# Routing constants in three parts, matrices ahead of a batch's scatters, seven first layers ahead

## The chip, the cores and the metric

The kernel runs on one core of a Trainium2 chip. A core has five engines that run side by side, each with its own instruction queue: TensorE (PE, matrix products and transposes), VectorE (DVE), ScalarE (ACT), GpSimd (POOL) and SyncE (SP, which here only issues transfers). Transfers (DMAs) are issued from POOL's, SP's and ACT's queues and run on 16 shared DMA engines. The metric is the device time of one execution in microseconds; less is better.

## The reference

Chunked attention with memory keys, followed by a mixture of experts with a dense residual. Sizes: 4 batches, 8 heads, 768 positions, head size 64; so 3072 tokens of 512 numbers; 8 experts with a hidden width of 512.

```python
for c in range(seq // 32):                       # chunks of 32 queries
    k_full = [mem_k (8 rows), k from 16 before the chunk to 8 behind it]
    a = softmax(q_c @ k_full.T / 8)
    out[c] = a @ v_full
x = out as [3072, 512]
y_dense = relu(x @ w1_dense) @ w2_dense
logits = x @ w_gate                              # 8 experts
e = argmax(logits); g = softmax(logits)[e]
y = y_dense + g * (relu(x @ w1[e]) @ w2[e])      # each token by its own expert e
```

## The kernel before

**Attention.** The loop runs over 16 pairs of heads (`NPAIR`), four pairs to a batch of 768 tokens. It is software-pipelined: in the iteration of pair i TensorE does the scores of pair i + 1, the transposes of pair i + 2 and the values of pair i; DVE does the maximum (L409), the subtraction (L415), the scaling of the values (`scaled`, L447 and L448), one copy of key columns (L376) and one of v's two head copies (L351); ScalarE does the exponential and PSUM copies; POOL does the other v copy and issues the loads of q and k. SyncE loads v.

The order on each engine is written out by hand: `tc.manual_schedule` keeps the instructions of each engine in the order in which the program calls them, and an instruction that waits holds up all that stands behind it on its engine.

**Routing.** As a batch's four pairs are done, its logits are summed up. In the second pair of the next batch (`routing`, pairs 5, 9 and 13) `logits`, `choose`, `ranks` and `rank` work out each token's expert and its row in a table in device memory, `x_reg`. Then POOL writes the batch's 768 rows there with six indirect DMAs of 128 rows (`rows_out`, L587), each one behind a tiny memset (`apart`, L578). Those of batches 0 and 1 are spread over later pairs by `row_out`; those of batch 2 come all at the end of pair 13, each followed by half a weight matrix (`half_w`); those of batch 3 come behind the attention (from "for t in range(T): rows_out(B - 1, (t,))"). The routing needs constants (ones, triangles, counters). `constants()` makes them at the end of the iteration of pair 1: DVE memsets (L733 to L747), POOL iotas (L122), and a DVE cast of each iota (L124), one by one.

**Tiles.** Tokens are processed in tiles of 128 that belong to one expert. In the last pair `list_a` works out the first 11 tiles (`NA`) from whole tiles of batches 0 to 2. SyncE reads their addresses into registers (`bases`) and fetches each from `x_reg` (`fetch`, L188); these fetches wait for the rows of batches 0 to 2, not for those of batch 3. `transposed` (L202 to L207) turns a tile, `dense_first` (L216, L222) and `dense_second` (L232, L235) do the dense layers. The other tiles (16, `NFIX`) are listed by `list_b` when batch 3's rows are placed, and follow in a second loop.

**Weights.** All matrices are loaded by POOL with a cast to 16 bits, in the order of `w_todo`: the two dense ones, then `w1` of the 8 experts, then `w2`. A `half_w` issues half a matrix (L779), `load_w` a whole one (L115). The last twelve are issued in a loop behind the rows of batch 3; there a tiny POOL copy (L964) waits until the matrix before the previous one has landed, so two are under way.

**Experts.** `experts(lo, hi, ahead)` runs for 27 tiles: `staged` copies the tile's `w1` matrix to a fixed place (DVE, L929), `expert_first` does the first layer, `expert_second` (L942, L947) the second, then POOL runs a memset of 256 numbers (`pause`, L581) and an indirect DMA (L951) that writes 128 rows of the output. The second layers read `w2` at a place known only at run time, so the first of them waits for all of `w2`. First layers run `ahead` of the second ones, by this formula:

```python
want = min(hi, lo + ahead + -(-(k + 1 - lo) * (hi - lo - ahead) // (hi - lo)))
```

Before the second layer of tile `k`, first layers up to `want` have been issued. Results `y` have a ring of 6 buffers, each free again when its output DMA has landed.

Of the kernel before, what the change touches and what calls it, by code (L numbers as in the profile page):

```python
# [11 lines left out]
F32 = mybir.dt.float32  # L12
# [8 lines left out]
def kernel(  # L21
# [90 lines left out]
    def load_w(src_ap, dst, parts=1):  # L112
        n = DT // parts
        for t in range(0, DT, n):
# [2 lines left out]
                src_ap[t * 128:(t + n) * 128].rearrange("(t p) m -> p t m", p=128),  # L117
            )

    def iota_f32(n, name, base=0, step=1, cm=0):  # L120
        ti = r_pool.tile([128, n], I32, name=name + "_i")
        nc.gpsimd.iota(ti, pattern=[[step, n]], base=base, channel_multiplier=cm)  # L122
        tf = r_pool.tile([128, n], F32, name=name)
        nc.vector.tensor_copy(tf, ti)  # L124
        return tf

    xT_A = keep.tile([128, NA, DT, 128], BF16, name="xT_A")
# [372 lines left out]
    def gate_add(pi):  # L500
        b, hp = divmod(pi, NP)
        lgT = bat[b]["lgT"]
        if hp == 0:
            nc.vector.tensor_copy(lgT, g_ps[:96, :])
        else:
            nc.vector.tensor_tensor(lgT, lgT, g_ps[:96, :], ALU.add)

    def logits(b):
        lgT = bat[b]["lgT"]
        lg_ps = bank()  # L510
        for j in range(2):
            nc.tensor.transpose(
                lg_ps[:, j * 96:(j + 1) * 96], lgT[:, j * 128:(j + 1) * 128],
                identity_f32[:96, :96],
            )
        bat[b]["lg"] = lg_ps
# [25 lines left out]
    def ranks(b):  # L542

        oh = bat[b]["oh"]
        rk_t = bank()
        rk_ps = rk_t[:, :T * E].rearrange("p (t e) -> p t e", e=E)
        nc.tensor.matmul(rk_ps, upper, oh, start=True, stop=False)
        for t in range(T - 1):
            nc.tensor.matmul(
                rk_ps[:, t + 1:, :], ones,  # L550
                oh[:, t:t + 1, :].to_broadcast([128, T - 1 - t, E]),
                start=False, stop=False,
            )
# [23 lines left out]
    def apart():  # L577
        nc.gpsimd.memset(scratch, 0.0)  # L578

    def pause():  # L580
        nc.gpsimd.memset(idle, 0.0)  # L581

    def rows_out(b, ts=range(T)):
        rec, row_i = bat[b]["rec"], bat[b]["row"]
# [142 lines left out]
        clear_v(i, nc.vector)  # L727
    load_v(2)

    def constants():  # L730
        out_ = {}
        ones = r_pool.tile([128, 128], BF16, name="ones")
        nc.vector.memset(ones, 1.0)  # L733
        upper = r_pool.tile([128, 128], BF16, name="upper")
        nc.gpsimd.affine_select(
            upper, ones, pattern=[[1, 128]], compare_op=ALU.is_ge, fill=0.0,
            base=-1, channel_multiplier=-1,
        )
        upto = r_pool.tile([128, E, E], F32, name="upto")
# [7 lines left out]
        nc.vector.memset(fill[:, IC:], FAR)  # L747
        slot_no = iota_f32(NB, "slot_no")
# [6 lines left out]
        reg0 = iota_f32(E, "reg0", base=128, step=ROWS)  # L755
        nc.vector.tensor_copy(seen_bf, reg25)
        return ones, upper, upto, slot_no, slot128, desc, pcol, tok, base_a, reg25, reg0

    transpose_qk(0)
    scores(0)  # L760
# [3 lines left out]
    copy_v(0, 0, nc.gpsimd)  # L764
    transpose_qk(1)
    copy_v(0, 1, nc.vector)
    probs_back(0)
    w_todo = [(moe_w1_dense, w1d_sb), (moe_w2_dense, w2d_sb)]
    for e in range(E):
# [15 lines left out]
    for i in range(NPAIR):  # L785
        b, hp = divmod(i, NP)
        routing = hp == 1 and b > 0
        if routing:
            gate_add(i - 2)
        if i + 4 < NPAIR:  # L790
            load_qk(i + 4, "q")
        if i + 3 < NPAIR:
            load_v(i + 3)
        if i + 1 < NPAIR:
            row_out()
            if i < NPAIR - 2:
                copy_v(i + 1, 0, nc.gpsimd)
            row_out()
            scores(i + 1)
        if i + 4 < NPAIR:  # L800
            load_qk(i + 4, "k")
        if i < 2:
            clear_side(i + 2, nc.gpsimd)
        if routing:
            logits(b - 1)
        if i:
            scaled(i - 1)
            copy_v(i, 1, nc.scalar if routing else nc.vector)
        if routing:
            choose(b - 1)  # L810
        if i:
            probs_back(i)
            gate_part(i - 1)
        if i + 1 < NPAIR:
            maximum(i + 1)
            softmax(i + 1)
        if i > 1 and not routing:
            gate_add(i - 2)
        if i == NPAIR - 1:
            parts = list_a()  # L820
            next(parts)
            bases(0, 6)
            for s in range(6):
                fetch(s)
            bases(6, NA)
        values(i, range(TB))
        if i + 2 < NPAIR:
            transpose_qk(i + 2)
        values(i, range(TB, T))
        if routing:  # L830
            ranks(b - 1)
        if i:
            record(i - 1)
            if i == NPAIR - 2:
                copy_v(i + 1, 0, nc.scalar)
            gate_sum(i - 1)
        if routing:
            rank(b - 1)
        if i == NPAIR - 4:
            half_w()  # L840
            half_w()
        if routing:
            rows_todo += [(b - 1, (t,)) for t in range(T)]
        if i == NPAIR - 3:
            while rows_todo:
                row_out()
                half_w()
        if i == 1:
            (ones, upper, upto, slot_no, slot128, desc, pcol, tok, base_a, reg25,
             reg0) = constants()  # L850
        if i == NPAIR - 3:
            fill_out()

# [6 lines left out]
    gate_sum(last_p)  # L860
    record(last_p)
    gate_add(last_p)
    transposed(0)
    logits(B - 1)
    dense_first(0)
    choose(B - 1)
    transposed(1)
# [3 lines left out]
    rank(B - 1)  # L871
    for t in range(T):
        rows_out(B - 1, (t,))
        if t < 2:
            half_w()
        elif t < T - 1:
            pause()
    dense_second(0)
    fetch(7)
# [57 lines left out]
    def expert_second(s):  # L937
        h_e = h_of.pop(s)
        place, py = y_bank()
        e = e_pe.pop(s)  # L940
        for f in range(FT):
            written(place, nc.tensor.matmul(  # L942
                py, h_e[:, f, :], w2_all[:, bass.ds(e, 1), f, :],
                start=(f == 0), stop=(f == FT - 1),
            ))
        y = l_work.tile([128, D_moe], F32, tag="y", name="y", bufs=6)
        was_read(place, nc.vector.scalar_tensor_tensor(  # L947
            y, py, meta[:, s:s + 1], yd_of[s], op0=ALU.mult, op1=ALU.add
        ))
        pause()  # L950
        inst = nc.gpsimd.indirect_dma_start(  # L951
            out, bass.IndirectOffsetOnAxis(ap=dst_i[:, s:s + 1], axis=0), y, None,
            bounds_check=N_tokens - 1, oob_is_err=False,
        )
        tc.declare_no_dep(inst.ins, group="outs", reason="every row is written once")
        tc.add_to_no_dep_group("outs", inst.ins)
# [41 lines left out]
            expert_second(k)  # L998

    turn["banks"] = 4  # L1000
    experts(0, last, NA)
    n_used = nc.values_load(  # L1002
        et_i[0:1, NS:NS + 1], min_val=0, max_val=NB,
        skip_runtime_bounds_check_because="a count of tiles",
# [40 lines left out]
```

## Time and profile before

| what | value |
|---|---|
| median of 3 runs | 251.78 us (249.72 to 254.38) |
| the profiled execution's own time | 251.12 us |
| its span, first to last instruction | 249.3 us |
| mean granted TensorE clock | 0.964 |
| busy PE / DVE / ACT / POOL | 198.0 / 157.6 / 135.0 / 146.5 us |
| moved by DMA | 38.57 MB, mean 155 GB/s |
| attention | to about 125 us |
| dense tiles | about 128 to 187 us |
| experts | about 187 us to the end |

Busy times are sums over a program whose stages have different limits, so none of them alone says what a change is worth; the stages and the waits within them do. TensorE's matmuls are pipelined, so its busy time is not time at its peak. The granted clock is the share of full speed that the chip let TensorE run at.

### The profile page before, as it was taken

To read this page: it belongs to the slowest core of one execution; us is meant where nothing else is said; L and a number is where in the kernel's file an instruction comes from. 1 tells how busy PE (TensorE), PEld (TensorE's weight loads), DVE (VectorE), ACT (ScalarE), POOL (GpSimd) and SP (SyncE) were. 2 spreads that over 40 slices of the span, in tenths; PEclk is the share of its full clock that TensorE was granted. 3 is DMA by queue.
4 is the path that set the end of the run, shared out by engine and by line. 5 is a ranking of instruction groups with operands and counts; after the bars stand their busy time and mean duration, and the time that the engine had idled before them with its cause. 6 is when DMAs were issued, how large, how long until landed. Compare 5 with 4: busy or idle time off the path is not lost. (4 is left out here: it accounts for less than half of the span.)

```text
span 249.3 us, 7849 instructions
## 1 busy us (share of the span) xinstructions
PE 198.0 (79%) x3147; PEld 147.8 (59%) x3147; DVE 157.6 (63%) x372; ACT 135.0 (54%) x205; POOL 146.5 (59%) x209
## 2 busy tenths in 40 slices
PE   1578498978887887686548998999999999998810
PEld 1466376756765665564336776777769866665500
DVE  4568679879888988877634542222236577887510
ACT  6265666896878667887314464566566512212100
POOL 8939973317996599428712841122131079988881
PEclk9999859999999999999988999999999999999985
DMA  5999999998999999948988959999989024332432
GB/s 91 184 193 134 160 157 158 148 146 158 167 172 202 163 139 170 164 163 122 212 187 158 203 84 245 234 196 203 145 138 163 6 84 168 148 137 113 163 127 87
DMA packets 59895, 38.57 MB, mean 155 GB/s; under 512 B 35662, under 2 KB 57550, under 8 KB 59856
## 3 DMA queue, kind: packets, MB, share of 16 engines
q0 software_dynamic: 21600, 25.20, 57.1%
q1 hardware_dynamic: 37216, 11.77, 28.4%
q10 hardware_dynamic: 1040, 1.06, 1.3%
q8 instruction: 27, 0.44, 0.8%
q14 instruction: 12, 0.10, 0.1%
HBM read 43.22 MB, written 11.30 MB: 219 GB/s over the span
## 5 line engine op out<-in xcount | busy, mean ns | idle before, releaser
L587 POOL DMA_INDIRECT x_reg<-rec,row_i x24 | 27.8, 1160 | 28.0 <-ACT rec L478 12.8
L951 POOL DMA_INDIRECT out_dram<-y,dst_i x27 | 30.0, 1113 | 17.0 <-DVE y L947 13.6
L436 PE MATMUL av<-vw,at 128*32 128x130 f32 x768 | 30.1, 292 | 8.3 <-issue 3.7
L436 PEld LDWEIGHTS av<-vw,at 128*32 128x32 f32 x768 | 21.4, 115 | 15.3 <-issue 10.0
L351 POOL COPY vw<-vw 24x1536 f32<-24x1536 f32 x15 | 22.5, 1500 | 13.2 <-DMA vw<-in_v_dram 12.7
L222 ACT ACTIVATE h<-sc 128x512 bf16<-128x512 f32 x27 | 16.1, 597 | 24.8 <-PE sc L216 22.9
L216 PEld LDWEIGHTS <-w_st 128*128 128x128 bf16 x432 | 25.3, 98 | 5.6 <-DVE w_st L929 1.7
L216 PEld LDWEIGHTS <-w1d 128*128 128x128 bf16 x432 | 26.3, 100 | 2.1 <-issue 1.7
L222 ACT ACTIVATE xT_B<-sc 128x512 bf16<-128x512 f32 x16 | 9.6, 597 | 28.8 <-PE sc L216 20.1
L420 ACT ACTIVATE a<-dif 128x768 f32<-128x768 f32 x16 | 13.5, 845 | 18.3 <-DVE dif L415 15.6
L929 DVE COPY w_st<-w_all 128x2048 bf16 x27 | 19.0, 709 | 6.3 <-PE sc L216 5.0
L205 DVE COPY xT_B<-tp 128x512 bf16<-128x512 bf16 x16 | 6.8, 425 | 24.1 <-PE tp L202 24.1
L376 DVE COPY kbd<-tp 64x768 bf16<-64x768 bf16 x16 | 15.2, 947 | 8.3 <-PE tp L363 7.3
L232 PE MATMUL av<-w2d,h 128*128 128x512 bf16 x72 | 18.5, 379 | 0.1
L964 POOL CAST scratch<-w_all 1x1 f32<-1x1 bf16 x10 | 1.7, 175 | 28.6 <-DMA w_all<-in_moe_w_dram 28.6
L468 PE MATMUL tp<-identity_f,x 128*128 128x128 f32 x96 | 14.1, 285 | 4.9 <-DVE x L448 4.8
L216 PE MATMUL sc<-xT_B,w_st 128*128 128x128 bf16 x256 | 16.9, 219 | 1.0 <-DVE w_st L929 0.6
L428 ACT COPY at<-at_ps 128x768 f32<-128x768 f32 x16 | 12.8, 799 | 9.0 <-PE at_ps L426 7.8
L471 ACT COPY xT<-tp 128x384 f32<-128x384 f32 x32 | 14.0, 488 | 6.2 <-PE tp L468 6.1
L409 DVE TENSOR_REDUCE mx<-sc 128x12 f32<-128x768 f32 x16 | 15.3, 956 | 2.8 <-PE sc L399 2.4
L216 PE MATMUL sc<-xT_B,w1d 128*128 128x128 bf16 x256 | 16.9, 219 | 0.0
L415 DVE TENSOR_TENSOR dif<-sc,mx 128x768 f32<-128x768 f32 x16 | 15.3, 958 | 1.6
(160 smaller groups left out, 450.2 us busy)
## 6 DMA issues: line engine op xcount, KB each, us to landing
w_all<-in_moe_w_dram POOLq DMA_DIRECT2D x13, 512.0 KB
vw<-in_v_dram SPq DMA_DIRECT2D x30, 200.0 KB
xg<-x_reg SPq DMA_DIRECT2D x27, 129.0 KB
q_bf<-in_q_dram POOLq DMA_DIRECT2D x16, 192.0 KB
k_bf<-in_k_dram POOLq DMA_DIRECT2D x16, 192.0 KB
vw<-in_mem_v_dram SPq DMA_DIRECT2D x32, 48.0 KB
w_all<-in_moe_w_dram POOLq DMA_DIRECT2D x6, 256.0 KB
x_reg<-fill ACTq DMA_DIRECT2D x1, 1032.0 KB
```

Of the source, the lines that this page charges most:

```text
L216: written(place, nc.tensor.matmul(ph[:, f, :], w[:, d, f * 128:(f + 1) * 128], xT[:, d, :], start=(d == 0), stop=(d == DT - 1),))
L222: was_read(place, nc.scalar.activation(h_sb, ph, AF.Relu))
L232: written(place, nc.tensor.matmul(pd, h_d[:, f, :], w2d_sb[:, f, :], start=(f == 0), stop=(f == FT - 1)))
L351: copy(vt[p0 + CHUNK:p0 + CTX, :NCH, hh, :D], vt[p0:p0 + n, 1:, hh, :D])
L376: lo = nc.vector.tensor_copy(dst[:D, 0], srcv[:D])
L409: nc.vector.reduce_max(mx, scv, axis=AX.X)
L415: nc.vector.tensor_tensor(dif.rearrange("p (b t) (h k) -> p b (t h) k", b=2, h=2), scv, mx.to_broadcast([128, 2, T, KEYS]), ALU.subtract,)
L436: nc.tensor.matmul(av[cc * CHUNK:(cc + 1) * CHUNK, t // TB, (t % TB) * W2:(t % TB + 1) * W2], at[:, t, cc * CHUNK:(cc + 1) * CHUNK], vt[:, ...
L468: nc.tensor.transpose(xtt[:, t * 128:(t + 1) * 128], xb[:, t0 + t, :], identity_f32)
L587: inst = nc.gpsimd.indirect_dma_start(x_reg, bass.IndirectOffsetOnAxis(ap=row_i[:, t:t + 1], axis=0), rec[:, t, :], None,)
L929: nc.vector.tensor_copy(w_st[:, None], w1_all[:, bass.ds(e_dve.pop(s), 1), :, :])
L951: inst = nc.gpsimd.indirect_dma_start(out, bass.IndirectOffsetOnAxis(ap=dst_i[:, s:s + 1], axis=0), y, None, bounds_check=N_tokens - 1, oo ...
```

## The change

It has five parts.

- `constants()` is cut in three. The memsets (`constants_set`) move to the first pair, ahead of its `probs_back`. The POOL part (one select and the iotas) stays at the end of pair 1. The casts (`constants_cast`) are collected and run in the iteration of pair 2, ahead of `record(1)`.
- In pair 13 six `half_w` (three matrices: the second dense one and two of `w1`) are issued on POOL ahead of `scores`. Behind the pair, the six scatters of batch 2 have a `pause` between them instead of a half matrix, and one whole matrix follows the last.
- The scatters of batch 3 have a `pause` between them throughout; before, half a matrix stood behind each of the first two. The matrix that `load_w` issues behind the attention is so one further in the list, and the loop of twelve is the same.
- `logits(B - 1)` is called ahead of `transposed(0)`.
- In the experts' stage the memset ahead of each output DMA covers 128 numbers instead of 256, and `ahead` is 7 instead of 11.

```diff
+    to_cast = []
     def iota_f32(n, name, base=0, step=1, cm=0):
         ...
-        nc.vector.tensor_copy(tf, ti)
+        to_cast.append((tf, ti))
...
-    def pause():
-        nc.gpsimd.memset(idle, 0.0)
+    def pause(n=256):
+        nc.gpsimd.memset(idle[:, :n], 0.0)
...
+    def constants_set():
         nc.vector.memset(ones, 1.0)
         ...
+    def constants():
+        nc.gpsimd.affine_select(upper, ones, ...)
         slot_no = iota_f32(NB, "slot_no")
         ...
+    def constants_cast():
+        for tf, ti in to_cast:
+            nc.vector.tensor_copy(tf, ti)
         nc.vector.tensor_copy(seen_bf, reg25)
...
     copy_v(0, 1, nc.vector)
+    constants_set()
     probs_back(0)
...
                 copy_v(i + 1, 0, nc.gpsimd)
+            if i == NPAIR - 3:
+                for _ in range(6):
+                    half_w()
             row_out()
             scores(i + 1)
...
             ranks(b - 1)
+        if i == 2:
+            constants_cast()
         if i:
             record(i - 1)
...
         if i == NPAIR - 3:
             while rows_todo:
                 row_out()
-                half_w()
+                if rows_todo:
+                    pause()
+            load_w(*w_todo.pop(0))
...
+    logits(B - 1)
     transposed(0)
-    logits(B - 1)
     dense_first(0)
...
         rows_out(B - 1, (t,))
-        if t < 2:
-            half_w()
-        elif t < T - 1:
+        if t < T - 1:
             pause()
...
-        pause()
+        pause(128)
         inst = nc.gpsimd.indirect_dma_start(out, ...)
...
-    experts(0, last, NA)
+    experts(0, last, 7)
```

More of the change, by code (lines that the diff above doesn't have):

```diff
@@ L728 @@
     load_v(2)
-    def constants():
-        out_ = {}
-        ones = r_pool.tile([128, 128], BF16, name="ones")
+    ones = r_pool.tile([128, 128], BF16, name="ones")
+    upper = r_pool.tile([128, 128], BF16, name="upper")
+    upto = r_pool.tile([128, E, E], F32, name="upto")
+    def constants_set():
         nc.vector.memset(ones, 1.0)
[L734 to L739, printed above, removed]
         nc.vector.memset(upto, 0.0)
@@ L747, in constants @@
         nc.vector.memset(fill[:, IC:], FAR)
+    def constants():
+        nc.gpsimd.affine_select(
+            upper, ones, pattern=[[1, 128]], compare_op=ALU.is_ge, fill=0.0,
+            base=-1, channel_multiplier=-1,
+        )
         slot_no = iota_f32(NB, "slot_no")
@@ L755, in constants @@
         reg0 = iota_f32(E, "reg0", base=128, step=ROWS)
+        return slot_no, slot128, desc, pcol, tok, base_a, reg25, reg0
+    def constants_cast():
+        for tf, ti in to_cast:
+            nc.vector.tensor_copy(tf, ti)
         nc.vector.tensor_copy(seen_bf, reg25)
-        return ones, upper, upto, slot_no, slot128, desc, pcol, tok, base_a, reg25, reg0
     transpose_qk(0)
@@ L846 @@
                 row_out()
-                half_w()
+                if rows_todo:
+                    pause()
+            load_w(*w_todo.pop(0))
         if i == 1:
-            (ones, upper, upto, slot_no, slot128, desc, pcol, tok, base_a, reg25,
-             reg0) = constants()
+            slot_no, slot128, desc, pcol, tok, base_a, reg25, reg0 = constants()
         if i == NPAIR - 3:
```

## The prediction

> **What bounds the kernel now.** I read the stages first (each engine's busy time per stretch), then each stage's waits, then the timeline of the engine that has none. Columns of a stretch: its bounds, its length, busy time of PE, weight loads, DVE, ACT, POOL (instruction counts in brackets), granted clock, DMA share, GB/s.
>
> ```profile
> 38.00:103.00 65.00, 53.19 (x1199) 40.78 (x1202) 56.84 (x96) 50.04 (x74) 43.86 (x52) 1.00 1.12 163
> 153.00:187.00 34.00, 33.07 (x390) 24.46 (x389) 10.11 (x50) 19.68 (x34) 8.22 (x18) 1.00 1.07 191
> ```
>
> Attention is DVE's (56.84 of 65 us), the dense tiles are TensorE's (33.07 of 34). The end is POOL's. In its timeline a row is start, duration, then the instruction, and in brackets the idle time before it:
>
> ```profile
> 200.80 1.26 POOL L951 DMA_INDIRECT out_dram<-y,dst_i  x1 [12.61 <-DVE y L947]
> ...
> 212.22 0.30 POOL L581 MEMSET idle<- 1x256 f32 x1
> 212.69 1.44 POOL L951 DMA_INDIRECT out_dram<-y,dst_i  x1 [0.17 <-issue]
> ...
> 243.23 0.99 POOL L951 DMA_INDIRECT out_dram<-y,dst_i  x1 [0.17 <-issue]
> ```
>
> The first output scatter waits for its data; the other 26 follow with only the memset and 0.17 us between. The chain that ended last lies in these scatters. From the first start to the last: 42.43 us. So four places can move the end: DVE in attention, whatever separates attention from the first dense tile, the dense tiles' TensorE, and when the first scatter starts and how fast 27 of them go.
>
> **1. The constants.** DVE's timeline at the end of the second pair:
>
> ```profile
> 25.92 0.17 DVE L733 MEMSET ones<- 128x128 bf16 x1
> ...
> 28.75 0.18 DVE L124 CAST slot_no<-slot_no_i 128x20 f32<-128x20 int32 x1 [1.89 <-POOL slot_no_i L122]
> ...
> 29.55 0.22 DVE L447 RECIPROCAL rs<-av 128x12 f32<-128x12 f32 x1
> ```
>
> From 25.92 to 29.55, 3.63 us, DVE does nothing for the pairs: 0.94 of memsets, 1.89 waiting for POOL's iotas, 0.80 of casts. All of it leaves this place. Who waited on it, and what DVE has to spare:
>
> ```profile
> PE tp L468 <- DVE x L448: 2.1, 1, 2.1
> ```
>
> ```profile
> DVE mx L409 <- PE sc L399: 1.6, 1, 1.6
> DVE rs L447 <- PE av L436: 0.5, 1, 0.5
> ```
>
> The memsets move ahead of the first pair's probabilities, just before the maximum that waits 1.6 for the scores: 0.94 fits, cost 0 (0.94 if that wait went). The iotas keep their place on POOL, where they are done by 28.75, before the casts now come. The casts come one pair later, right before the reciprocal that waited 0.5 for TensorE: they fill 0.5 and push 0.3. ScalarE's token column, which reads one of them in that pair, stands behind its copies and finds it done. Gain 3.63 - 0.3 = **3.3**. Bounds: 4.1 if TensorE's delay in that pair (below) also goes and buys DVE its other wait, 2.1 if only TensorE's own wait is won.
>
> ```profile
> 30.00:32.00 2.00, 1.09 (x5) 1.12 (x6) 1.97 (x2) 0.13 (x1) 1.99 (x2) 0.50 1.41 135
> ```
>
> TensorE's clock is 0.50 just behind its 2.1 us wait; without the wait I expect 1.00 here. The Trainium skill speaks against that ("TensorE: Matmul & The Clock Gate", the table "Why this matters for your kernels"): only idle gaps above about 3 us cost the clock. By it the half clock has another cause and stays, and the sum would be an estimated 1.2 us less, by the lower bound above. The trace has the drop after a gap of 2.1, so the row decides.
>
> **2. The third batch's scatters and the first fetch.**
>
> ```profile
> 110.92 1.52 POOL L587 DMA_INDIRECT x_reg<-rec,row_i  x1 [8.40 <-ACT rec L478]
> ...
> 122.00 1.05 POOL L587 DMA_INDIRECT x_reg<-rec,row_i  x1 [0.23 <-issue]
> ...
> 142.49 0.98 POOL L587 DMA_INDIRECT x_reg<-rec,row_i  x1 [0.17 <-issue]
> 143.96 0.98 POOL L587 DMA_INDIRECT x_reg<-rec,row_i  x1 [0.17 <-issue]
> ```
>
> ```profile
> SPq L188 <- DMA x_reg<-rec,row_i: 3.4, 1, 3.4
> ```
>
> ```profile
> 126.45 3.00 SPq L188 DMA_DIRECT2D xg<-x_reg  x6
> ```
>
> ```profile
> 128.64 0.47 PE L202 MATMUL tp<-identity,xg 128*128 128x128 bf16 x4 [3.37 <-DMA xg<-x_reg]
> 128.91 0.53 PE L512 MATMUL tp<-identity_f,lgT 96*128 96x96 f32 x2
> 129.63 1.87 PE L216 MATMUL sc<-xT_A,w1d 128*128 128x128 bf16 x16 [0.19 <-DVE xT_A L205]
> ...
> 199.49 1.06 PE L216 MATMUL sc<-xT_B,w_st 128*128 128x128 bf16 x16
> ```
>
> With a half matrix behind each scatter the six start 11.08 us apart, 2.22 a step; with a memset between, the last two show 1.47. Five steps at 1.47 plus the first's longer 1.52: the last scatter starts 3.2 us sooner. SyncE had waited 3.4 for it, the whole delay of the first fetch, which issues at 126.45 and lands 2.2 later. TensorE lost 3.37 there, from 125.27. With the fetch 3.2 earlier the tile lies ready at 125.4. TensorE now does the logits (0.53) first, and these want a last sum from DVE, for which I allow 0.4; so it takes the tile at 126.2 instead of 128.64, 2.4 won. Its first dense layer took 1.87 after the long wait against 1.06 for the same sixteen matmuls at 199.49; warm, that is 0.8 more, and 0.3 for the transposes at its side. Together **3.5**; bounds 0 (the rows land no sooner) and 3.9.
>
> Where the matrices went: six half loads (256 KB each by their shape) issue on POOL in front of the scatters. One costs at most 2.22 - 1.47 + 0.30 = 1.05 of POOL's time, six 6.3, within the 8.40 it sat idle, so no scatter waits for their issue. Their 1.5 MB meet DMA engines that lie idle for part of it:
>
> ```profile
> 106.00:108.00 2.00, 1.53 (x48) 1.33 (x48) 0.87 (x1) 1.98 (x5) 0.00 (x0) 1.00 0.08 14
> ```
>
> If that cover were gone, they would lie in front of the scatters in POOL's own queue: that is rival B. SyncE's queue is not touched: the next transfers it issues are these fetches. The whole matrix issued behind the sixth scatter shares the DMA engines with the fetch, as halves did before.
>
> **3. The last batch.** Two half loads between its scatters become memsets: two steps shrink by up to 0.75, so the second list's fetches and the twelve remaining loads start up to 1.5 sooner. What waited for those fetches:
>
> ```profile
> PE tp L202 <- DMA xg<-x_reg: 0.9, 2, 0.8
> ```
>
> Gain **0.9**, bounds 0 and 1.2.
>
> **4. Seven first layers ahead.**
>
> ```profile
> 187.04 10.33 PE L216 MATMUL sc<-xT_A,w_st 128*128 128x128 bf16 x176
> ...
> 198.63 1.02 PE L942 MATMUL av<-w_all,xT_A 128*128 x4 [0.36 <-issue]
> ```
>
> By the code's formula 8 first layers now precede the first second layer, not 12. 176 matmuls are 11 layers, 0.93 a layer: the first scatter comes 3.7 earlier. That moves four staging copies behind the first scatter: 18, not 14.
>
> ```profile
> L929 DVE COPY w_st<-w_all x14: 678/682/881, 200.4 to 233.3; 128x2048 bf16 x14
> ```
>
> ```profile
> L578 POOL MEMSET scratch<- 1x1 f32 x24 | 2.9, 120 | 0.5
> ```
>
> A clean step is 0.99 + 0.30 + 0.17 = 1.46; 26 make 37.9, and the 4.5 us left of 42.43 are 14 copies at 0.32 (the scatter at 212.69, beside one, took 1.44). The half-size memset lies between 0.12 for one element and 0.30 for 256: about 0.21, saving 0.09 (bounds 0, if the scatter takes it back, and 0.15). New: 26 x 1.37 + 18 x 0.32 = 41.4. TensorE needs 19 first layers at 0.93 and 26 second layers at 0.86 (198.63 to 199.49), 40.0, so POOL stays the bound, narrowly. Gain 3.7 + 1.0 = **4.7**; bounds 2.4 (no gain from the memset: 3.7 - 4 x 0.32) and 6.3 (0.15 a step).
>
> The Trainium skill ("SBUF — State Buffer", "Who interferes with whom") has a rule against this step: a DVE copy in a two-port mode holds the port it shares with GpSimd for the whole instruction and the loser fully blocks. By it each copy would cost its 0.68; rival D prices it.
>
> **Sum:** 3.3 + 3.5 + 0.9 + 4.7 = 12.4, from the profiled execution's 251.12: **238.7**. That run is 0.66 below the median of three that span 4.66, so I add nothing.
>
> **The rivals.** A: the pairs are paced by transfers, not DVE (DMA share 1.12 in the first row). Step 1 is worth nothing: 242.0. Against it: none of DVE's waits quoted is for a DMA. Chance 0.08.
>
> B: the change does not free the rows: 1.5 MB ahead of them in the same queue make the last scatter land when it did. Step 2 is lost: 242.2. For it: the moved loads and the scatters share POOL's queue; against: the empty stretch at 106. Chance 0.10.
>
> C: the second weights come too late.
>
> ```profile
> 193.00:194.00 1.00, 1.00 (x21) 1.00 (x19) 0.73 (x2) 0.64 (x2) 0.00 (x0) 1.00 0.12 19
> ```
>
> The DMA share falls to 0.12 at 193, so the last of the w2 loads has landed; the first second layer came at 198.63, 5.6 later. Now it comes at 198.63 - 7.7 - 3.7 = 187.2, and the loads must have moved by the same 7.7 to leave 1.9. If they stay at 193, it waits 5.8: 244.5. Chance 0.10.
>
> D: the full port lock, 0.68 a copy: 18 x 0.36 = 6.5 more, 245.2. The 0.32 of the old stage speaks against it: 0.03.
>
> E, the slower side: the same wait, with the loads slower than before. The loop starts behind the last scatter's end (144.94) and finished twelve loads by 193, 4.0 each; its slowest step:
>
> ```profile
> 156.13 0.17 POOL L964 CAST scratch<-w_all 1x1 f32<-1x1 bf16 x1 [2.90 <-DMA w_all<-in_moe_w_dram]
> ```
>
> ```profile
> 161.45 0.17 POOL L964 CAST scratch<-w_all 1x1 f32<-1x1 bf16 x1 [4.12 <-DMA w_all<-in_moe_w_dram]
> ```
>
> 5.32. Twelve at that, plus one step for the two in flight, end at 137.2 + 69.2 = 206.4, and 2.2 to the scatter, 41.4, and the 7.9 from the last scatter's start to the end make 257.9. It decides against the change from a landing at 199.6. Chance 0.07.
>
> **How the numbers follow.** Forecast 238.7: 0.57. Two of A to D at once, about 247: 0.05. Some 2% (5 us) is what a measurement of this kernel tells from no change. Faster by more: 0.57 + 0.08 + 0.10 + 0.10 + 0.03 = 0.88; within: 0.05 and 0.02 of E, 0.07; slower: 0.05. The range runs from all upper bounds (15.5 won, 235.6) to rivals C and D: 235 to 245.5.
>
> **What would show it.** Step 1: no DVE gap of 1.9 near 28, clock 1.00 at 30. Step 2: SyncE's wait for x_reg under 1 us, TensorE's wait before its first tile under 1. Step 3: no wait of TensorE for xg near 150. Step 4: eight first layers before the first second layer, no DMA wait there, scatter steps of 1.37. The forecast is wrong if w2 lands after the eighth first layer, or if DVE's 3.3 us return as waits for loads.

## The result

The changed kernel took 239.85 us (238.85 to 240.54, 4 runs) beside 251.58 us (249.72 to 254.38, 4 runs) for the kernel before: ratio 0.9554, 95% interval 0.9482 to 0.9626. The prediction was 238.7. A second measurement, on another chip, gave 240.95 against 250.66: 0.9633, 0.9552 to 0.9714. So the change is worth 9.7 to 11.7 us. The profiled execution took 238.85 us, 12.27 less than the profiled one of before; I follow these 12.27 from stage to stage. Ratios leave out the executions that took over 1.5% longer than the fastest of their kernel; in three kernels below (early fill, memset of 256, two matrices) the profiled execution was such a one, and from those I read single waits and stages alone.

The chain that ended last, in shares of the span, by engine and by line, of the changed kernel:

```profile
POOL 23%; DMA 20%; issue 9%; PE 5%; DVE 5%; ACT 4%; POOLq 1%; ACTq 0%; DVEq 0%
DMA w_all<-in_moe_w_dram 16%; POOL out_dram L964 12%; POOL x_reg L589 5%; POOL idle L583 4%; DMA x_reg<-rec,row_i 2%; DMA xg<-x_reg 2%; PE sc L218 1%; ACT kbd L379 1%; DVE dif L417 1%; DVE mx L411 1%; DVE x L450 1%; DVE kbd L378 1%; ACT qT L374 1%; PE tp L470 1%; PE av L438 1%
```

The output scatters (L964, formerly L951) still end it. Ahead of them the chain follows POOL's own queue back through its weight loads, 16%. That doesn't make the loads the cause: POOL issued the last of them at 179.73 and then stood until the first scatter at 190.21, which waited for its data (9.55 us, step 4 below).

**Step 1, the constants.** DVE's timeline of the changed kernel (start, duration, instruction), the end of the second pair and of the third:

```profile
25.04 0.94 DVE L378 COPY kbd<-tp 64x768 bf16<-64x768 bf16 x1
25.90 0.21 DVE L449 RECIPROCAL rs<-av 128x12 f32<-128x12 f32 x1
...
32.40 0.34 DVE L764 CAST slot_no<-slot_no_i 128x20 f32<-128x20 int32 x1
...
33.11 0.37 DVE L449 RECIPROCAL rs<-av 128x12 f32<-128x12 f32 x1
```

The second pair's reciprocal starts at 25.90 instead of 29.55, with nothing between the copy and it; the casts take 0.71 us, 32.40 to 33.11. In the last pair it starts 5.97 sooner, which is more than the 3.63 us that left the second pair. The same row in four executions: before, the experts' change alone, the constants alone, and the changed kernel.

```profile
121.76 0.22 DVE L447 RECIPROCAL rs<-av 128x12 f32<-128x12 f32 x1
```

```profile
119.08 0.22 DVE L447 RECIPROCAL rs<-av 128x12 f32<-128x12 f32 x1
```

```profile
116.10 0.23 DVE L449 RECIPROCAL rs<-av 128x12 f32<-128x12 f32 x1
```

```profile
115.79 0.23 DVE L449 RECIPROCAL rs<-av 128x12 f32<-128x12 f32 x1
```

The second execution has the attention code of before, letter for letter, and is 2.68 shorter; in two more with the constants at their old place the row starts at 118.80 and 119.13. So the profile that I predicted from had a long attention, and against the others the constants are worth 119.08 - 116.10 = 2.98 to 119.08 - 115.79 = 3.29 us in these two executions. They don't keep that everywhere. The third pair's reciprocal starts at 36.65 to 37.17 with the old constants and at 32.96 to 33.16 in four of the ten executions with the new ones, but at 34.18 to 36.81 in the other six, the second profile of the changed kernel (34.18) among them. In these TensorE was late in the third pair and DVE waited for its transposes, the longest time in the run with the memset of 256:

```profile
34.99 0.95 DVE L378 COPY kbd<-tp 64x768 bf16<-64x768 bf16 x1 [3.53 <-PE tp L365]
```

There the last reciprocal starts at 119.03, as with the old constants. The last section comes back to this.

The stretches that decide, with the columns as in the prediction:

```profile
30.00:32.00 2.00, 2.00 (x69) 1.71 (x65) 1.85 (x4) 1.30 (x4) 1.95 (x2) 1.00 0.96 157
...
120.00:122.00 2.00, 0.58 (x2) 0.29 (x2) 0.21 (x1) 0.00 (x0) 0.00 (x0) 0.50 1.10 266
...
186.00:187.00 1.00, 0.94 (x17) 0.76 (x14) 0.69 (x1) 0.62 (x2) 0.00 (x0) 1.00 0.05 7
```

The clock at 30 is 1.00, no longer 0.50. At 120, ahead of the first tile, it is 0.50.

**Step 2, the first fetch.** SyncE's wait, two pieces of the chain in order of time (start, length, what), and TensorE's timeline, all of the changed kernel:

```profile
SPq L190 <- DMA x_reg<-rec,row_i: 1.1, 1, 1.1
```

```profile
113.30 4.94 DMA x_reg<-rec,row_i
...
118.25 3.81 DMA xg<-x_reg
```

```profile
117.15 0.84 PE L470 MATMUL tp<-identity_f,x 128*128 128x128 f32 x6 [2.02 <-DVE x L450]
...
122.10 0.61 PE L204 MATMUL tp<-identity,xg 128*128 128x128 bf16 x4 [1.26 <-DMA xg<-x_reg]
123.22 1.86 PE L218 MATMUL sc<-xT_A,w1d 128*128 128x128 bf16 x16 [0.52 <-DVE xT_A L207]
...
179.39 7.55 PE L218 MATMUL sc<-xT_A,w_st 128*128 128x128 bf16 x128
188.04 1.02 PE L955 MATMUL av<-w_all,xT_A 128*128 x4 [1.10 <-issue]
```

The scatters went nearly as forecast: measured from the last reciprocal, the last one starts 2.73 us sooner than before (forecast 3.2). But from its start to the landing of its rows pass 4.94 us instead of 4.45 (122.00 to 126.45), and the fetch lands 3.81 behind its issue instead of 2.2, so that only 0.57 of the 2.73 is left when TensorE takes the tile. The first dense layer takes 1.86 as before, at half clock; the clock had fallen to 0.50 by 119, ahead of the wait for the tile. The layer starts 123.22 - 115.79 = 7.43 behind the last reciprocal, against 129.63 - 121.76 = 7.87: 0.44 won of 3.5.

**Step 3.** From the first dense layer to the first expert layer: 179.39 - 123.22 = 56.17, before 187.04 - 129.63 = 57.41. Won 1.24 in this execution. TensorE's wait for the second list's tiles fell from 0.9 us to 0.3, but the stage's length varies by more than that: the same code took 57.25 in the changed kernel's second profile.

**Step 4.** Eight layers precede the first second layer (128 matmuls), but TensorE idles 1.10 ahead of it instead of 0.36, and the DMA share falls to 0.05 only at 186. The profile names no releaser here; that TensorE waited for the last of `w2` is read from these two. From the first expert layer to it 8.65 us instead of 11.59, 2.94 won of 3.7. POOL's timeline:

```profile
190.21 1.25 POOL L964 DMA_INDIRECT out_dram<-y,dst_i  x1 [9.55 <-DVE y L960]
191.45 0.19 POOL L583 MEMSET idle<- 1x128 f32 x1
...
230.66 0.98 POOL L964 DMA_INDIRECT out_dram<-y,dst_i  x1 [0.17 <-issue]
```

The scatters take 40.45 instead of 42.43, so 1.98 won. A clean step is 0.98 + 0.19 + 0.17 = 1.34, 26 of them 34.8, and 5.6 are left for 18 copies: 0.31 each.

The account: 5.97 (of it 2.7 not the change's) + 0.44 + 1.24 + 2.94 + 1.98 - 0.30 (last scatter to end, 8.19 instead of 7.89) = 12.27. Without the 2.7 it is 9.6.

### The profile page after: what moved, and what is told of

Read it like the earlier page. It is cut to its first block, busy times and chain, and to the rows that moved or that the text cites. A ratio compares the mean times of both kernels' runs of the same rounds, so it can differ in the third digit from the quotient of the medians.

```text
span 237.0 us, 7850 instructions
## 1 busy us (share of the span) xinstructions
PE 195.5 (82%) x3147; PEld 146.3 (62%) x3147; DVE 157.2 (66%) x372; ACT 135.0 (57%) x205; POOL 145.1 (61%) x215
## 4 chain that ended last, share of the span: by engine, by line
POOL 23%; DMA 20%; issue 9%; PE 5%; DVE 5%; ACT 4%; POOLq 1%; ACTq 0%; DVEq 0%
DMA w_all<-in_moe_w_dram 16%; POOL out_dram L964 12%; POOL x_reg L589 5%; POOL idle L583 4%; DMA x_reg<-rec,row_i 2%; DMA xg<-x_reg 2%; PE sc L218 1%; ACT kbd L379 1%; DVE dif L417 1%; DVE mx L411 1%; DVE x L450 1%; DVE kbd L378 1%; ACT qT L374 1%; PE tp L470 1%; PE av L438 1%
## 5 line engine op out<-in xcount | busy, mean ns | idle before, releaser
L589 POOL DMA_INDIRECT x_reg<-rec,row_i x24 | 26.7, 1111 | 20.7 <-ACT rec L480 12.5
L964 POOL DMA_INDIRECT out_dram<-y,dst_i x27 | 29.0, 1074 | 14.3 <-DVE y L960 10.6
L438 PE MATMUL av<-vw,at 128*32 128x130 f32 x768 | 29.1, 284 | 8.5 <-issue 3.9
L438 PEld LDWEIGHTS av<-vw,at 128*32 128x32 f32 x768 | 20.7, 112 | 15.6 <-issue 6.5
L218 PEld LDWEIGHTS <-w_st 128*128 128x128 bf16 x432 | 25.5, 98 | 5.8 <-DVE w_st L942 3.2
L218 PEld LDWEIGHTS <-w1d 128*128 128x128 bf16 x432 | 26.2, 100 | 2.2 <-issue 1.8
L942 DVE COPY w_st<-w_all 128x2048 bf16 x27 | 19.9, 740 | 5.6 <-PE sc L218 4.1
L218 PE MATMUL sc<-xT_B,w_st 128*128 128x128 bf16 x256 | 16.9, 219 | 0.2 <-DVE w_st L942 0.2
L218 PE MATMUL sc<-xT_B,w1d 128*128 128x128 bf16 x256 | 16.9, 219 | 0.0
L450 DVE TENSOR_TENSOR x<-av,rs 128x768 f32<-128x768 f32 x16 | 15.3, 958 | 0.6
```

The lines of the kernel that those rows point to most:

```text
L218: written(place, nc.tensor.matmul(ph[:, f, :], w[:, d, f * 128:(f + 1) * 128], xT[:, d, :], start=(d == 0), stop=(d == DT - 1),))
L438: nc.tensor.matmul(av[cc * CHUNK:(cc + 1) * CHUNK, t // TB, (t % TB) * W2:(t % TB + 1) * W2], at[:, t, cc * CHUNK:(cc + 1) * CHUNK], vt[:, ...
L450: nc.vector.tensor_tensor(x_p.rearrange("p (b t) (h d) -> p b (t h) d", b=2, h=2), avv[:, :, :, :D], rs.to_broadcast([128, 2, TB * 2, D]), ...
L589: inst = nc.gpsimd.indirect_dma_start(x_reg, bass.IndirectOffsetOnAxis(ap=row_i[:, t:t + 1], axis=0), rec[:, t, :], None,)
L942: nc.vector.tensor_copy(w_st[:, None], w1_all[:, bass.ds(e_dve.pop(s), 1), :, :])
L964: inst = nc.gpsimd.indirect_dma_start(out, bass.IndirectOffsetOnAxis(ap=dst_i[:, s:s + 1], axis=0), y, None, bounds_check=N_tokens - 1, oo ...
```

## The experiments

Two questions: is each term what I took it for, measured by itself, and what took the place of the wait in step 2? The kernel before in the three series took 250.25 (13 runs), 250.66 (7) and 249.56 us (7); a ratio is against the one of its own series.

| kernel | us | ratio, 95% interval | transposes to layer | last scatter to tile |
|---|---|---|---|---|
| constants alone | 247.35 | 0.9896, 0.9800 to 0.9993 | 7.55 | 7.06 |
| scatters alone | 248.97 | 0.9962, 0.9909 to 1.0014 | 6.36 | 9.10 |
| experts alone | 245.67 | 0.9834, 0.9736 to 0.9933 | 7.49 | 7.01 |
| all but the constants | 244.15 | 0.9772, 0.9677 to 0.9868 | 7.90 | 10.62 |
| changed, again | 240.95 | 0.9633, 0.9552 to 0.9714 | 6.34 | 9.05 |
| matrix later | 236.90 | 0.9466, 0.9395 to 0.9537 | 3.92 | 6.57 |
| warm TensorE | 240.72 | 0.9601, 0.9527 to 0.9675 | 6.19 | 9.14 |
| fill early | 243.27 | 0.9691, 0.9595 to 0.9787 | 5.28 | 8.00 |
| memset of 256 | 245.89 | 0.9810, 0.9748 to 0.9872 | 8.11 | 10.84 |
| two matrices behind | 246.05 | none given (241.42 to 246.88) | 10.35 | 13.08 |
| matrix later, 5 ahead | 241.87 | 0.9646, 0.9581 to 0.9711 | 5.39 | 8.26 |
| matrix later, logits behind | 238.81 | 0.9579, 0.9519 to 0.9639 | 4.88 | 7.53 |

The last two columns are step 2's own measures in the profiled execution. The first is the time from the start of the last pair's transposes (the row L470 above, L468 in kernels with the old constants) to the start of the first dense layer (L218, L216). It was 6.51 in the profile before, 6.07 in that of the changed kernel, and should have become about 3. The second is the time from the start of the sixth scatter of batch 2 to TensorE's first instruction on the first tile: 6.64 before, 8.80 in the changed kernel. The first four kernels ran on one chip, the next four on a second, the last four on a third.

### One part at a time

**The constants alone**: the change with its scatters, logits and experts undone.

```diff
-            if i == NPAIR - 3:
-                for _ in range(6):
-                    half_w()
...
-    logits(B - 1)
     transposed(0)
+    logits(B - 1)
...
-        pause(128)
+        pause()
...
-    experts(0, last, 7)
+    experts(0, last, NA)
```

> Only the constants are cut in three; all else as before. The prediction's step 1: 3.3 us less, about 248.3 of 251.6, with the reciprocals of all later pairs 3.7 or so earlier and no more. Rival, from the trace of the changed kernel (the last pair's reciprocal 6.0 us earlier, the third pair's only 3.8): the pairs behind the third give 1 to 2 us more, also with nothing else changed, so 5 to 6 us less, about 246. If the reciprocals of pairs 9 to 12 are 3.7 earlier and not 4.5 to 5.1, the extra is not the constants' work.

2.6 us less by the ratio, and the last reciprocal at 116.10 (above), near the changed kernel's 115.79. Part of the gain comes back at the fetch, where the rows now are later than the attention; SyncE's wait:

```profile
SPq L190 <- DMA x_reg<-rec,row_i: 4.2, 1, 4.2
```

3.4 in the profile before. That fits step 1's size, though the interval alone would allow anything from 0.2 to 5 us; the rest of the 5.97 was the earlier profile's own.

**The scatters alone**: the matrices and memsets around the scatters of batches 2 and 3, all else as before.

```diff
+            if i == NPAIR - 3:
+                for _ in range(6):
+                    half_w()
...
                 row_out()
-                half_w()
+                if rows_todo:
+                    pause()
+            load_w(*w_todo.pop(0))
...
-        if t < 2:
-            half_w()
-        elif t < T - 1:
+        if t < T - 1:
             pause()
```

> Only the scatters of the third and last batch and the matrices around them are changed; constants, logits and the experts' stage as before. The prediction's steps 2 and 3: 3.5 + 0.9 = 4.4 us less, about 247.2, TensorE warm at its first dense tile. Rival, from the trace of the changed kernel: the whole matrix issued right behind the sixth scatter delays the landing of the rows and the first fetch, and the clock falls all the same: 0.4 + 1.2 = 1.6 us less, about 250, the fetch landing some 3.8 us after its issue instead of 2.2.

1.0 us less by the ratio, within what ten runs can tell from nothing. SyncE's waits and TensorE's timeline at the tile:

```profile
SPq L188 <- DMA x_reg<-rec,row_i: 1.2, 1, 1.2
SPq L188 <- DMA x_reg<-fill: 1.0, 1, 1.0
```

```profile
125.74 0.61 PE L202 MATMUL tp<-identity,xg 128*128 128x128 bf16 x4 [2.66 <-DMA xg<-x_reg]
...
126.86 1.86 PE L216 MATMUL sc<-xT_A,w1d 128*128 128x128 bf16 x16 [0.20 <-DVE xT_A L205]
```

Two waits have come in place of one: for the rows, and for `fill`, the 1 MB that ScalarE's queue writes over `x_reg`'s free rows at the end of pair 13. The fetch issues at 122.57 and lands 3.1 us later. TensorE still waits 2.66 for the tile and its first layer is at half speed. Step 2 falls short without any help from the other parts.

**The experts alone.**

```diff
-        pause()
+        pause(128)
...
-    experts(0, last, NA)
+    experts(0, last, 7)
```

> Only the experts' stage: 7 first layers ahead, memsets of 128. The prediction's step 4: 4.7 us less, about 246.9, the first second layer 3.7 us earlier. Rival: the first second layer waits for the last of w2, and only 2.9 of the 3.7 is won; the scatters themselves give 2.0 instead of 1.0: 4.9 less in all, about 246.7, but the idle time in front of the first second layer is 1.1 us instead of 0.4.

4.2 us less by the ratio. TensorE's and POOL's timelines:

```profile
186.07 7.52 PE L216 MATMUL sc<-xT_A,w_st 128*128 128x128 bf16 x128
193.92 1.02 PE L942 MATMUL av<-w_all,xT_A 128*128 x4 [0.33 <-issue]
```

```profile
196.09 1.26 POOL L951 DMA_INDIRECT out_dram<-y,dst_i  x1 [8.95 <-DVE y L947]
...
236.54 0.98 POOL L951 DMA_INDIRECT out_dram<-y,dst_i  x1 [0.17 <-issue]
```

Here `w2` is there in time: 7.85 us from the first expert layer to the second layer, the whole 3.7 won. The scatters take 40.45, the same as in the changed kernel. So in the changed kernel's first profile 0.8 of this gain went to the 1.10 us of idle time; in its second the figure is 7.85 too.

**All but the constants**, logits included; the diff is the change without its first part.

> The changed kernel with the constants put back at the end of the second pair. If the parts add up, it is slower than the changed kernel by what the constants alone give: 3.3 us by the prediction (243.2), 5 to 6 us by the rival (245 to 246).

5.7 us less by the ratio. Against the changed kernel's two ratios it is 3.5 to 5.5 us slower, which lies between the two forecasts and rules out neither. The fetch's wait for the fill is at its longest here:

```profile
SPq L188 <- DMA x_reg<-fill: 4.2, 1, 4.2
```

The three parts alone make 2.6 + 1.0 + 4.2 = 7.8, and the whole by its ratios 9.2 to 11.2: they agree within their intervals, which are too wide to rule out 1 to 3 us from how the parts meet.

### What took the place of the wait

**The changed kernel again**, beside the next three on one chip.

> The changed kernel once more, on the chip of the three beside it, as their measure: about 240. In its profile the first fetch again waits for the third batch's rows or for the fill rows, and TensorE's first dense layer takes 1.86 us at half clock.

```profile
SPq L190 <- DMA x_reg<-fill: 2.5, 1, 2.5
```

```profile
123.43 0.61 PE L204 MATMUL tp<-identity,xg 128*128 128x128 bf16 x4 [1.51 <-DMA xg<-x_reg]
124.56 1.86 PE L218 MATMUL sc<-xT_A,w1d 128*128 128x128 bf16 x16 [0.52 <-DVE xT_A L207]
...
127.36 1.87 PE L218 MATMUL sc<-xT_A,w1d 128*128 128x128 bf16 x16 [0.51 <-DVE xT_A L207]
```

Here the fill ends last, not the rows, and two first layers run at half speed.

**The matrix later**: the whole matrix behind the sixth scatter is issued where the next one is, when the second tile has landed.

```diff
                 row_out()
                 if rows_todo:
                     pause()
-            load_w(*w_todo.pop(0))
...
     nc.gpsimd.tensor_copy(scratch, xg_of[1][0:1, 0:1])
     load_w(*w_todo.pop(0))
+    load_w(*w_todo.pop(0))
```

> The changed kernel with the whole matrix not issued right behind the sixth scatter but with the next one, when the second tile has landed. Theory: that matrix shares the DMA engines with the rows, the fill rows and the first fetch; without it the fetch issues up to 1.1 us sooner and lands 2.2 instead of 3.8 us later: 1.3 us less than the changed kernel, as TensorE's wait is no longer (1.26). Rival: the six halves ahead of the scatters are what holds the rows; then the landing of the rows does not move and nothing is won.

236.90 us (235.81 to 237.37), 4.05 less than the changed kernel beside it (240.08 to 242.18). SyncE's wait and TensorE's timeline:

```profile
SPq L190 <- DMA x_reg<-fill: 0.7, 1, 0.7
```

```profile
118.20 0.85 PE L470 MATMUL tp<-identity_f,x 128*128 128x128 f32 x6 [1.97 <-DVE x L450]
...
121.21 0.40 PE L204 MATMUL tp<-identity,xg 128*128 128x128 bf16 x4
122.12 1.05 PE L218 MATMUL sc<-xT_A,w1d 128*128 128x128 bf16 x16 [0.51 <-DVE xT_A L207]
```

In both profiles the last pair's transposes start at 118.2. Then the wait for the fill is 0.7 instead of 2.5, TensorE waits for no tile, and its first layer takes 1.05 and starts 2.44 sooner. This is what step 2 forecast, and the edit shows which of its steps was wrong: 512 KB of load behind the scatters were not free. The dense tiles then take 55.14 instead of 57.25 (from 122.12 to 177.26, and from 124.56 to 181.81), another 2.1, at a clock that stays at 1.00. This version is the fastest of all.

Two runs further down have the same edit, on the third chip, and there the tile was not in time: SyncE waited 2.3 and 1.5 us for the fill, TensorE 1.43 and 1.82 for the tile. So the matrix is a part of the delay and not all of it. Its share is read chip by chip, from the last scatter to the tile: 9.05 and 9.14 with it and 6.57 without on the second chip, 10.84 with it and 7.53 and 8.26 without on the third, so 2.5 to 3.3 us. What delays the fill and the rows in the two late runs stays open; the six halves ahead and the fill itself are both still there.

**Two matrices behind**: the opposite dose, a second whole matrix behind the sixth scatter and none behind the second tile.

```diff
             load_w(*w_todo.pop(0))
+            load_w(*w_todo.pop(0))
...
     nc.gpsimd.tensor_copy(scratch, xg_of[1][0:1, 0:1])
-    load_w(*w_todo.pop(0))
```

> The changed kernel with a second whole matrix right behind the first one behind the sixth scatter (the one that otherwise waits for the second tile). Theory: transfers issued there delay the rows, the fill rows and the first fetch; with twice as many TensorE's wait before its first tile grows from 1.3 to 1.5 by another 1 to 3 us, at half clock. Rival: it was the order of the loads behind, not their weight at this place; then the wait is the same 1.3 to 1.5 us.

```profile
129.08 0.61 PE L204 MATMUL tp<-identity,xg 128*128 128x128 bf16 x4 [6.18 <-DMA xg<-x_reg]
130.20 1.86 PE L218 MATMUL sc<-xT_A,w1d 128*128 128x128 bf16 x16 [0.52 <-DVE xT_A L207]
```

From the last scatter to the tile 13.08 us pass, 2.2 more than with one matrix on the same chip (10.84). TensorE's wait for the tile is 6.18 with two matrices behind the scatters, 1.26 to 2.74 in four executions with one (the changed kernel twice, warm TensorE, memset of 256), and 0 to 1.82 in three with none; the last two ranges overlap, but not on one chip. The times of its runs scatter too much for a ratio.

**The fill early**: the fill is written at the end of the sixth pair.

```diff
-        if i == NPAIR - 3:
+        if i == 5:
             fill_out()
```

> The changed kernel with the 1 MB of fill rows written at the end of the sixth pair instead of the fourteenth. Theory: the moved matrices meet this write, and the first fetch waits for it or for the rows behind it; written early it leaves the stretch, the rows land 1 to 2 us sooner, the fetch issues without a wait, and the kernel is up to 1.3 us faster. Rival: the write costs the pairs as much at its new place (ratio within 0.5% of the changed kernel).

The first fetch waits no more for the fill and TensorE only 0.46 for the tile, though its first layer still takes 1.87. The kernel is no faster for it (0.9691 against 0.9633, intervals that overlap). The 1 MB meets the loads of the pairs instead: SyncE's loads of v stand still for 10.0 us behind it (51.6 to 61.6), DVE then waits 2.0 for one of them, and two pairs, from reciprocal to reciprocal, take 16.24 us (65.33 to 81.57) where the changed kernel beside it takes 14.14. Not all of that need be the fill's, as the run with two matrices has two pairs as slow there (16.66). At the end TensorE idles longer ahead of the second layers:

```profile
192.74 1.85 PE L955 MATMUL av<-w_all,xT_A 128*128 x4 [2.44 <-issue]
```

The fill costs something at either place; that one of the two is better isn't shown.

**TensorE kept warm**: fourteen more matmuls, read by nothing, around the logits.

```diff
+    warm(8)
     scaled(last_p)
...
+    warm(2)
     logits(B - 1)
+    warm(4)
     transposed(0)
```

> The changed kernel with 14 matmuls more that nothing reads, in the gaps in front of TensorE's first tile (8 behind the last pair's gate products, 2 and 4 around the logits). Theory: the clock falls because TensorE idles 2.0 us there and little stands around it; with the fillers it stays 1.00 and the first two tiles are 1.0 to 1.4 us faster: 1 us less in all. Rival: the clock falls for another reason, the first layer still takes 1.86 us, and the fillers cost up to 1 us.

```profile
125.17 0.40 PE L204 MATMUL tp<-identity,xg 128*128 128x128 bf16 x4 [1.37 <-DMA xg<-x_reg]
126.08 1.86 PE L218 MATMUL sc<-xT_A,w1d 128*128 128x128 bf16 x16 [0.52 <-DVE xT_A L207]
```

240.72 against 240.95: nothing. The clock holds up to the tile's transposes (0.40 for four, as at full clock) and the first layer behind them is at half speed all the same. The wait for the tile alone doesn't explain it: with the matrix later and the logits behind, a wait of 1.82 is followed by a layer of 1.05. Warming up bought nothing here, and what makes the clock fall stays open.

### The experts' sizes and the logits

**The memset of 256 again**, in the changed kernel.

```diff
-        pause(128)
+        pause(256)
```

> The changed kernel with the memset of 256 numbers back in front of each output DMA. Theory: POOL paces the 27 scatters, so each step is longer by the 0.10 to 0.11 us that the memset takes more, and from the first scatter to the last it is 26 x 0.11 = 2.8 us more (43.2 instead of 40.4); about 1.1% slower than the changed kernel. Rival: TensorE paces them (40.0 us of layers by the prediction), and not more than 1 us is lost.

```profile
196.75 1.25 POOL L964 DMA_INDIRECT out_dram<-y,dst_i  x1 [8.43 <-DVE y L960]
197.98 0.30 POOL L583 MEMSET idle<- 1x256 f32 x1
...
240.14 0.98 POOL L964 DMA_INDIRECT out_dram<-y,dst_i  x1 [0.17 <-issue]
```

The scatters take 43.39 instead of 40.45: 2.94, or 0.11 for each of 26 steps, so the memset's whole difference lies on the path. The clean step is 1.45, and 43.39 - 26 x 1.45 leaves 5.7 for 18 copies, again 0.32 each. (Its whole time is 6.0 above the changed kernel's first measurement, but on another chip, with a late third pair and a wait of 2.74 for the tile; the stage is the clean reading.)

**Five ahead instead of seven**, with the matrix later.

```diff
-    experts(0, last, 7)
+    experts(0, last, 5)
```

> As the run with the matrix issued later, but with 5 first layers ahead of the second ones. Theory: the first second layer there came 7.85 us behind the last dense one and the last w2 load landed about 2 us before it; two layers fewer use that up, and the end comes 1.2 us sooner (2 x 0.93 less 2 copies at 0.31), or not at all sooner where w2 lands late. Rival: w2 is what the first second layer waits for, and nothing is won.

```profile
122.17 0.40 PE L204 MATMUL tp<-identity,xg 128*128 128x128 bf16 x4 [1.43 <-DMA xg<-x_reg]
```

The tile is late here in spite of the matrix issued later, and the first layer takes 1.70. In the experts' stage six first layers precede, but TensorE then idles 1.11 us ahead of the second layers, and the scatters take 42.65 (188.89 to 231.54), 2.2 more than with seven: two copies more lie among them, and behind the first scatter POOL waits seven times for a `y` instead of four. What a smaller number wins at the start it gives back on the way.

**The logits behind the first tile again**, with the matrix later.

```diff
-    logits(B - 1)
     transposed(0)
+    logits(B - 1)
```

> As the run with the matrix issued later, but with the logits behind the first tile's transposes again. Theory: the logits fill a wait; put back they cost nothing to 0.4 us, within what can be measured. Rival: without them TensorE waits longer for the tile, the clock falls to half, and the first layers take 1.86 us: 1 us more.

```profile
123.52 0.40 PE L204 MATMUL tp<-identity,xg 128*128 128x128 bf16 x4 [1.82 <-DMA xg<-x_reg]
...
124.43 1.05 PE L218 MATMUL sc<-xT_A,w1d 128*128 128x128 bf16 x16 [0.34 <-DVE xT_A L207]
```

Ratio 0.9579 against 0.9466 with the logits ahead, with intervals that overlap and on different chips. TensorE waits 1.82 for the tile and the layer still runs at full speed, so the logits ahead are not what keeps the clock up; whether they are worth anything by themselves stays open.

## Why the prediction was right, point by point

Forecast 12.4 us, measured 9.7 to 11.7. The time was right, but one term was nearly lost, two were larger than forecast, and the two profiles that I compare flattered the change by 2.7. The terms as measured add up to 9.6. That the time came within 1.2 us of 238.7 with step 2 almost missing is in part luck: the kernel before took 251.58 beside the first measurement, and 249.6 to 250.7 in the later series.

- **What bounds each stage**: right. DVE's wait for the constants, the wait for the first tile and POOL in the scatters each moved the end when they were touched; TensorE in the dense tiles was not touched by itself. Rival A falls: the attention shortened by about what DVE lost, with the constants alone too.
- **Step 1**: right in its place, and in its size where the third pair ran without delay, 3.0 to 3.3 for 3.3. In six of ten executions part of it, or all, came back as a wait of DVE for TensorE in the third pair, which the prediction doesn't have. The clock at 30 is 1.00 in the changed kernel, but the 2.1 us gap isn't shown to have halved it: all but the constants keeps that gap (2.10) and has 1.00 at 30, and the second profile of the changed kernel has 0.50 at 31 without it.
- **Step 2**: wrong in size, 0.4 for 3.5. The scatters came sooner nearly as worked out. The step that failed is that rows and fetch land as quickly as before whatever lies behind them ("shares the DMA engines with the fetch, as halves did before"): from the last scatter to the tile 8.80 and 9.05 us passed instead of 6.64. One 512 KB load in the rows' own queue accounts for about that much: where it was taken away, the tile came 2.5 to 3.3 us sooner. I had listed what was queued ahead of the rows (rival B) and not what ran beside them: the fill, which the fetch came to wait for, is not named in the prediction at all. The second step that failed is the full clock at the first layer (1.1 of the 3.5): it was at half before the wait for the tile began, and why is not known. The same code varies here, too: 6.51, 7.55 and 7.49 from the transposes to the layer with the old order, 6.07 and 6.34 with the new.
- **Rival B** has its result, and for the larger part not its place: the halves are still ahead where the matrix comes later, and there the tile comes 2.5 to 3.3 us sooner, once in time. Whether they hold the rows in the two executions where it still came late isn't shown.
- **Step 3**: right in its place, as TensorE's wait for these tiles fell from 0.9 to 0.3. Its size is not pinned: the stage shortened by 1.24 in one profile and 0.16 in the other, for 0.9.
- **Step 4, the start**: 3.74 by itself as forecast, 2.94 in the changed kernel's profile. The difference is probably a small rival C: the loads came 0.8 late. In the second measurement of the same kernel the idle is 0.33, so it is on the edge and not always paid.
- **Step 4, the scatters**: the term was mis-sized, 1.98 for 1.0. The memset saves 0.11 a step instead of 0.09, and the clean step's scatter is 0.98, not 0.99. A copy costs 0.31 to 0.32 with 14 and with 18 of them.
- **Rival D** falls in its price: less than half of a copy's 0.68 is lost, in three kernels. The lock itself is there, as in the changed kernel where a copy (DVE) ends at 196.82 and POOL's memset, 0.19 when alone, began in the middle of it and ended 0.13 later:

```profile
195.90 0.92 DVE L942 COPY w_st<-w_all 128x2048 bf16 x1
```

```profile
196.29 0.66 POOL L583 MEMSET idle<- 1x128 f32 x1
```

  The Trainium skill ("SBUF — State Buffer", "Who interferes with whom") has the engine that comes second fully blocked, and this trace agrees. But POOL waits only for the rest of a copy that it meets, and a copy that lies within one scatter can cost nothing (200.37 to 201.05 beside a scatter of 0.98).
- **Rival E** falls: in the changed kernel's two profiles the loop was 0.8 late at most, not 8.

## What to carry to other kernels

When a wait for a transfer is to go, list everything that shares the DMA engines in that stretch, from every queue, and not only what stands ahead in its own; a load that nobody needs yet is best issued when the urgent transfer has landed. Sizing one instruction between two measured ones and counting the clean steps gave the scatters' time to 1 us. A profile is one execution: another kernel with the same code in a stage shows how far that stage varies by itself.

## What was not expected of the hardware

- **The clock.** Ahead of the last pair's transposes TensorE waits about 2 us in most executions, and what follows is not set by that wait: after 2.02 (the changed kernel) and 1.93 (the experts alone) the six gate matmuls behind the transposes (L495, L493 in kernels with the old constants) took 1.45, at half clock; after 1.97 (matrix later), 1.93 (the constants alone) and 2.22 (before) they took 1.01. After fourteen extra matmuls, a gap of 1.37 and one of 0.52 were followed by half clock. The Trainium skill ("TensorE: Matmul & The Clock Gate", "Why this matters for your kernels") warns of gaps above about 3 us; here the clock fell after shorter ones, and the length of one gap doesn't decide. What does stays open: idle time summed over a longer stretch is a guess that no run here tests.
- **A halt of TensorE in the third pair.** In seven executions (constants alone, changed again, matrix later, warm, memset of 256, 5 ahead, logits behind) it stops for 1.2 to 2.6 us between two transposes of a group, with no releaser that the profile shows; here in the last of these:

```profile
27.23 0.49 PE L470 MATMUL tp<-identity_f,x 128*128 128x128 f32 x3
30.02 0.49 PE L470 MATMUL tp<-identity_f,x 128*128 128x128 f32 x3 [2.31 <-issue]
```

It is in seven of the ten executions with the constants moved, not in the first profile of the changed kernel, and in none of the four with the constants at their old place. In six of the seven the third pair's reciprocal comes 1.0 to 3.9 us later than in the other executions with the new constants, up to the whole gain of step 1. Whether the new place of the constants brings the halt about is not shown, and its cause stays open.
